# Plain first-layer units for six block units, six H tiles, and another order of second-layer products in a fused attention and mixture kernel

## The chip, the core and the metric

The kernel runs on one core of a Trainium2 chip. The metric is the device time of one execution in microseconds. Five runs of the kernel before gave a median of 374.88 us, from 374.55 to 375.29. One execution was also recorded by the hardware profiler; the profile and the trace are of that one.

## The reference: what is computed

Two stages follow each other. The first is attention of 4 batches x 8 heads x 768 positions x 64, where each query sees the first 4 positions (the sink) and a window of the last 128 positions. The second is a mixture of 4 experts over the 3072 tokens: each expert is a two-layer network 512 -> 1024 -> 512, and its output is weighted with a normalised gate.

```python
scores = np.where(is_sink | in_window, scale * q @ k.T, -1e9)
x = softmax(scores) @ v                 # then heads side by side: [3072, 512]
p = domain_probs / domain_probs.sum(-1)
for e in range(4):
    out += p[:, e:e + 1] * (np.maximum(x @ w1[e], 0.0) @ w2[e])
```

## The kernel before, in words

**Tiling.** Tokens are worked on in groups of 256 (three groups for each batch, `NG = 3`). A *unit* is the first layer of one expert on one group: 48 units in all. Its result is a tile `H` (1024 hidden values x 256 tokens in bf16).

**A plain unit** (`emit_first`, L1001) has four steps. A step is eight matmuls of 128 x 128 weights on 256 token columns into one PSUM bank, `hps`; then one VectorE instruction (L1025) applies ReLU and the gate. In batch 0, L1014 on ScalarE or L1016 on VectorE does the ReLU alone.

**A block unit** (`emit_fast`, L1078) does the same with seven block products P1 to P7 in place of eight, in the manner of Strassen and Winograd: each is eight matmuls of 128 x 128 weights on 128 columns, into `cps`, so 56 in all. It works with sums and differences of weight blocks (`weight_form1`, L319 to L325, four VectorE instructions for each expert, once) and of token blocks (`tokens`, L1052). Its partial results are copied by ScalarE (L1106, L1119), added by VectorE (L1113, L1128) and gated by VectorE (L1097, four times). `START` says from which batch on an expert uses block units: expert 0 from batch 1, expert 1 from batch 2, experts 2 and 3 in batch 3. That makes 21 block units and 27 plain ones.

**The second layer** in batch 0 is plain (L1286). In batches 1 to 3 it too is done in seven block products for each group (`emit_product`, L1218). A product consists of one *piece* for each expert, four matmuls of 256 columns each; so a group's chain is 28 pieces. The products of a group come in the order of `CHAIN`. Two PSUM banks `acc` are used: P1, P6, P7 and P4 go to bank 0, P2, P5 and P3 to bank 1. Behind a product its bank is copied or added to the output tile `osb` by ScalarE (L1259) or VectorE (L1250, L1255), and P1 is copied to bank 1 (L1247). `S` holds the sums of H blocks that P5 and P6 need (L1178, three VectorE instructions for each unit), and L1157 forms the operand of P3. Each half of the output rows is stored by one DMA on SP's queue (L1236, L1252).

**What sets the order.** The kernel is written out by a planner that runs at build time: it keeps estimated times of the engines, and the loop at L1344 chooses the next TensorE work among those that are ready, by a priority number (lower first): attention that is due 0, otherwise 3; first-layer steps 2 (L1386); a product piece 1 or 2.5 (L1385). In before a piece gets 1 when VectorE is estimated to be more than `BEHIND` = 800 ns behind. Work of VectorE and ScalarE goes through a list with deadlines (`later`, `flush`).

**H tiles.** There are six H tiles (`NH`). When the last batch's attention is out, `widened` (L897) makes three more from the tile `qkT`, which the attention no longer needs. A tile is given back as soon as its expert's piece of the chain's last product is out (L1224). `room` tells whether another unit may be opened.

**Attention.** Scores of two head pairs go out in one burst when four of six PSUM banks are free (`two`, L777, with `PAIR = 1`), and sink scores of two query groups in one burst (L570, with `ONE = 2`).

Of the kernel before, what the change touches and what calls it, by code (L numbers as in the profile page):

```python
# [16 lines left out]
def kernel(  # L17
# [12 lines left out]
    nc = tc.nc  # L30
# [27 lines left out]
    ]  # L58

    NGATE = 5  # L60
    START = {0: 1, 1: 2, 2: 3, 3: 3}
    ONACT = 1
    ONE = 2
    PAIR = 1
    BEHIND = 800
    BIASED = 1
    FAST = tuple(START)
    UNITS = ("P1", "P5", "P6", "P2", "P7", "P3", "P4")
# [235 lines left out]
    def weight_form1(e):  # L304

        w = w1_sb[e].rearrange("p (k d) (m f) -> p m k d f", k=2, m=2)
        A11, A12, A21, A22 = w[:, 0, 0], w[:, 0, 1], w[:, 1, 0], w[:, 1, 1]
        if e not in forms1:
            if START[e] < B - 1:
                x = wpool.tile([P, 3, NDB // 2, F // 2], BF16, name=f"vf_{e}", tag=f"vf_{e}")  # L310
                x = [x[:, i] for i in range(3)]
            else:
                x = [sb.tile([P, 2, H, D], BF16, name="qkn", tag="qkn", bufs=NQB) for _ in range(3)]
                x = [i.rearrange("p d h c -> p d (h c)") for i in x]
            forms1[e] = {"P1": A11, "P2": A12, "P3": x[2], "P4": A22, "P5": x[0], "P6": x[1], "P7": A21}
            formed1[e] = 0
        x = forms1[e]
        if formed1[e] == 0:
            nc.vector.tensor_add(x["P5"], A21, A22)  # L319
        elif formed1[e] == 1:  # L320
            nc.vector.tensor_sub(x["P6"], x["P5"], A11)
        elif formed1[e] == 2:
            nc.vector.tensor_sub(x["P3"], A12, x["P6"])
        else:
            nc.vector.tensor_sub(A21, A11, A21)  # L325
        formed1[e] += 1
        forms1_at[e] = dve(1024, rate=1.92)
# [3 lines left out]

    def form1_due(e):
        n = formed1.get(e, 0)
        if START[e] == B - 1 and turned_at.get((B - 1, NQB - 1), 1e12) > t["pe"]:
            return False
        return landed.get(("w1", e), 1e12) < t["pe"] and (n < 3 or n == 3 and not left1[e])

    def form_due(e):
# [516 lines left out]
    NH = 6  # L855
    QF = NFB // 2
    PAIRS = [(b, g) for b in range(1, B) for g in range(NG)]
    CHAIN = ("P1", "P2", "P6", "P5", "P7", "P3", "P4")
    acc_free = [0.0, 0.0]
    out_sb = {}  # L860

    class Mixture:


        def __init__(self):
            self.early = {g: list(range(E)) for g in range(NG)}
# [12 lines left out]
            self.H, self.H_at, self.H_part = {}, {}, {}  # L879
            self.S, self.S_at, self.waiting, self.last = {}, {}, [], []  # L880
            self.products = [(b, g, m) for b, g in PAIRS for m in CHAIN]
            self.piece, self.chores = 0, 0
            self.at, self.S4_at, self.C22 = {}, {}, {}
            self.done = 0.0
            self.stored = []
            self.spare, self.lent = [], {}

        def is_fast(self, b, e):
            return b >= START.get(e, B)
# [1 line left out]
        def more(self):  # L891
            return bool(self.open or any(self.early.values()) or self.units or self.second or self.products)

        def room(self):
            return self.spare or self.live < NH

        def widened(self):  # L897

            x = sb.tile([P, 2, NHP, S], BF16, name="qkT", tag="qkT", bufs=1)
            x = x.rearrange("p i h n -> p (i h n)")  # L900
            n = 2 * QF * 2 * P
            self.spare = [x[:, i * n:(i + 1) * n].rearrange("p (k f t n) -> p k f t n", k=2, f=QF, t=2) for i in range(3)]

        def early_ready(self, g):
            if not self.early[g] or not self.room():
                return 1e12
            xs = [xT_at.get((0, hp, g), 1e12) for hp in range(NHP)]
            e = self.early[g][0]
            return max([t["pe"], free_at(), landed.get(("w1", e, 0), landed.get(("w1", e), 1e12)), *xs])

        def opened(self, b, g, e):

            if self.spare:
                self.H[b, g, e] = self.spare.pop()
                self.lent[b, g, e] = self.H[b, g, e]
            else:
                self.H[b, g, e] = mo.tile([P, 2, QF, 2, P], BF16, name="H", tag="H", bufs=NH)
                self.live += 1
            fast = self.is_fast(b, e)

            def complete(at):
                self.H_at[b, g, e] = at
                self.finished.add((b, g, e))
                if b:
                    self.waiting.append((b, g, e))
                    load_gates()

            self.H_part[b, g, e] = join(4, complete)
            return {"unit": (b, g, e), "fast": fast, "left": list(UNITS) if fast else list(range(QF)), "at": {}}

        def begin(self):

            if self.open or any(self.early.values()):
                return
            if self.units and self.room():
                self.open.append(self.opened(*self.units.pop(0)))

        def widen(self):

            u = self.open[0]  # L940
            if len(self.open) == 1 and u["unit"][0] and len(u["left"]) < len(UNITS) and self.units and self.room():
# [195 lines left out]
        def chore(self):  # L1137
# [11 lines left out]

            if self.last:  # L1150
                b, g, e = u = self.last[0]
                if (b, g, "P2") not in self.products:
                    self.last.pop(0)

                    def form(engine):
# [53 lines left out]
        def emit_product(self):  # L1209
# [11 lines left out]
                )  # L1221
            end = pe(QF * G, ready, n=QF)
            self.piece = (k + 1) % E
            if m == CHAIN[-1]:  # L1224
                if (b, g, e) in self.lent:
                    self.spare.append(self.lent.pop((b, g, e)))
                else:
                    self.live -= 1
            if k < E - 1:
                return  # L1230
            self.products.pop(0)
            if m == "P1":
                out_sb[b, g] = mo.tile([P, 2, Dout], FP32, name="osb", tag="osb", bufs=1)
                r = (b * NQB + 2 * g) * P
                def store(at):
                    nc.sync.dma_start(out=out[r + P:r + 2 * P, :], in_=out_sb[b, g][:, 1])  # L1236
                    sp(at)
                self.C22[b, g] = join(2, store)
            o = out_sb[b, g]
            C11, C12, C21, C22 = o[:, 0, 0:G], o[:, 0, G:], o[:, 1, 0:G], o[:, 1, G:]  # L1240
            acc_free[bank], seeded = 1e12, acc_free[1]
            if m == "P1":
                acc_free[1] = 1e12

            def run(engine):
                if m == "P1":
                    nc.scalar.copy(out=acc[1][:, 0:G], in_=x)  # L1247
                    acc_free[0] = acc_free[1] = act(G, seeded)
                elif m == "P3":
                    nc.vector.tensor_add(C12, C12, x)  # L1250
                    acc_free[1] = at = dve(G)
                    nc.sync.dma_start(out=out[r:r + P, :], in_=o[:, 0])  # L1252
                    sp(at)
                elif m == "P7":
                    nc.vector.tensor_add(C22, C22, x)  # L1255
                    acc_free[0] = at = dve(G)
                    self.C22[b, g](at)
                else:
                    nc.scalar.copy(out={"P2": C11, "P6": C12, "P5": C22, "P4": C21}[m], in_=x)  # L1259
                    acc_free[bank] = at = act(G)  # L1260
                    if m == "P4":
                        self.C22[b, g](at)
            r = (b * NQB + 2 * g) * P
            later("dve" if m in ("P3", "P7") else "act", end, 200, run)

        def second_ready(self):
            if not self.second:
# [53 lines left out]
    ahead, upto, loaded, wide = 0, 0.0, 0, 0  # L1321
# [22 lines left out]
    while mix.more() or att.more():  # L1344
        now = t["pe"]

        if not att.more() and ahead == B - 1 and not wide:
            wide = 1
            mix.widened()
        if not att.more() and not loaded:  # L1350
            loaded = 1
            gates_by_row()
# [28 lines left out]
        if att.more():  # L1381
            opts = [(max(r, now), (0 if due else 3) - 0.1 * (step == "two"), "att", step) for r, step in att.options()]
        s2, p = mix.second_ready(), mix.product_ready()
        behind = max(t["dve"] - now, 0.0) + 500 * sum(x[2] == "dve" and x[0] < now + 300 for x in pend)
        opts.append((max(p, now), 1 if behind > BEHIND else 2.5, "product", None))  # L1385
        opts += [(max(f, now), 2, "first", x) for f, x in mix.firsts()]  # L1386
        opts.append((max(s2, now), 1 if mix.since >= 1 else 2.5, "second", None))
        soonest = min(o[0] for o in opts)
# [58 lines left out]
```

The softmax here doesn't subtract the row's maximum and nothing guards it: scores larger than these inputs give would overflow.

## Time and profile before

| what | us |
|---|---|
| median of five runs | 374.88 |
| the profiled execution | 374.97 |
| its span, first to last instruction | 373.3 |
| TensorE busy / VectorE busy / ScalarE busy | 362.7 / 285.2 / 153.1 |
| L1001, plain first layer, 864 matmuls, busy | 107.0 |
| L1078, block first layer, 1176 matmuls, busy | 79.2 |
| L1218, second-layer products, 1008 matmuls, busy | 127.3 |
| last first-layer matmuls start | 349.73 |
| last DMA issued | 370.33 |

Times in the trace are counted from the start of the span. "PE" is TensorE's matmuls, "PEld" its weight loads, which overlap them, "DVE" VectorE, "ACT" ScalarE and "POOL" GpSimd. A busy time of a matmul is longer than the step from one matmul to the next, since matmuls are pipelined; the pace is read from starts. A bracket at the end of a timeline line tells how long the engine was idle before it and who ended that. In the view by windows, the columns are: the window, its length, then busy time and instructions of each engine, the granted TensorE clock, the DMA share and GB/s.

Attention runs beside the mixture until about 253 us; its last score burst starts at 240.84. From 281.5 to 350.2 come the first-layer units of batch 3 mixed with second-layer products, and from 350.17 second-layer products alone. The span ends 3.0 us after the last DMA is issued.

### The profile page before, as it was taken

The numbers are of one execution on the slowest core, as the hardware profiler recorded it, in microseconds if no ns is written. First come the engines' busy times: TensorE is split into PE (matmuls) and PEld (weight loads), VectorE is DVE, ScalarE is ACT, GpSimd is POOL, SyncE is SP. The second block draws the span as 40 slices with busy tenths as digits, with TensorE's granted clock in tenths as the row PEclk, the third lists the DMA queues.
The fourth block names the chain that finished last, engine by engine and source line by source line (L and its number), as shares of the span: only waits on it lengthen the run. The fifth ranks groups of instructions, "written<-read, shape, count | busy, mean of one in ns | idle before, by whom it ended". The sixth has DMA issues, their size and how long they took to land.

```text
span 373.3 us, 9793 instructions
## 1 busy us (share of the span) xinstructions
PE 362.7 (97%) x4096; PEld 300.2 (80%) x4096; DVE 285.2 (76%) x630; ACT 153.1 (41%) x396; POOL 71.1 (19%) x91
## 2 busy tenths in 40 slices
PE   6899999999999999999999999999999999999996
PEld 3575766667667788889987998899999999999975
DVE  5674997675553899778879789779899889899930
ACT  4764733675565226445336145543103222222110
POOL 8935112808131191001020000000000000000000
PEclk9999999999999999999999999999999999999999
DMA  9999999939999999027991023114012111110011
GB/s 164 165 189 199 210 211 177 149 25 119 136 129 211 159 139 129 30 70 73 167 147 43 3 64 80 41 45 86 16 30 72 30 44 58 31 59 2 2 56 58
DMA packets 110808, 35.63 MB, mean 95 GB/s; under 512 B 94260, under 2 KB 106132, under 8 KB 110764
## 3 DMA queue, kind: packets, MB, share of 16 engines
q0 software_dynamic: 77520, 17.31, 52.1%
q1 hardware_dynamic: 32188, 17.18, 20.8%
q8 instruction: 32, 0.52, 0.6%
q10 hardware_dynamic: 1056, 0.52, 0.5%
q14 instruction: 12, 0.10, 0.1%
HBM read 40.45 MB, written 6.34 MB: 125 GB/s over the span
## 4 chain that ended last, share of the span: by engine, by line
PE 88%; DVE 4%; ACT 4%; DMA 3%; issue 1%; ACTq 0%; DVEq 0%
PE acc L1218 29%; PE hps L1001 24%; PE cps L1078 17%; PE acc L1286 9%; PE sps L618 3%; PE od L684 2%; DMA xT<-onat 2%; DMA kraw<-in_k_dram 2%; PE tr L512 1%; ACT aT L643 1%; ACT onat L723 1%; PE od L677 1%; DVE H L1016 1%; DVE onat L714 1%; PE tx L742 1%
## 5 line engine op out<-in xcount | busy, mean ns | idle before, releaser
L1001 PE MATMUL hps<-xT,w 128*128 128x256 bf16 x864 | 107.0, 273 | 0.4 <-DVE H L1016 0.3
L1001 PEld LDWEIGHTS <-w 128*128 128x128 bf16 x864 | 82.2, 98 | 13.3 <-issue 2.5
L1218 PEld LDWEIGHTS <-H 128*128 128x128 bf16 x600 | 56.1, 98 | 7.6 <-issue 1.9
L643 ACT ACTIVATE aT<-sps 128x512 bf16<-128x512 f32 (+1 forms) x96 | 47.1, 576 | 30.7 <-PE sps L618 30.6
L723 ACT ACTIVATE onat<-od,R 128x64 bf16<-128x64 f32 x144 | 33.3, 331 | 39.7 <-DVE R L711 39.7
L1218 PE MATMUL acc<-w,H 128*128 128x256 bf16 x360 | 47.7, 272 | 1.0 <-ACT osb L1259 0.5
L1025 DVE SCALAR_TENSOR_TENSOR H<-hps,gates 128x512 bf16<-128x512 f32 x56 | 38.2, 689 | 12.4 <-PE hps L1001 12.2
L1286 PE MATMUL acc<-w,H 128*128 128x512 bf16 x192 | 45.4, 379 | 0.0
L1078 PEld LDWEIGHTS <-w 128*128 128x128 bf16 x672 | 42.5, 98 | 1.9 <-issue 0.5
L254 POOL DMA_DIRECT2D vx<-in_v_dram x24 | 21.4, 901 | 75.2 <-PE od L684 66.4
L1259 ACT COPY osb<-acc 128x256 f32<-128x256 f32 x36 | 13.6, 384 | 52.8 <-PE acc L1218 51.9
L1097 DVE SCALAR_TENSOR_TENSOR H<-cps,gates 128x512 bf16<-128x512 f32 x48 | 32.9, 687 | 2.1 <-PE cps L1078 1.3
L1286 PEld LDWEIGHTS <-H 128*128 128x128 bf16 x192 | 18.3, 98 | 17.5
L1218 PE MATMUL acc<-wf,H 128*128 128x256 bf16 x240 | 31.9, 273 | 0.0
L1014 ACT ACTIVATE H<-hps 128x512 bf16<-128x512 f32 x35 | 20.9, 598 | 24.2 <-PE hps L1001 23.8
L1218 PEld LDWEIGHTS <-S 128*128 128x128 bf16 x288 | 27.0, 98 | 3.8 <-issue 1.1
L1106 ACT COPY cps<-cps 128x512 f32<-128x512 f32 x21 | 12.1, 576 | 42.2 <-PE cps L1078 40.5
L1298 DVE SCALAR_TENSOR_TENSOR osb<-acc,scale_t,osb 128x512 f32<-128x512 f32 x18 | 13.5, 750 | 16.9 <-PE acc L1286 16.9
L1078 PE MATMUL cps<-T,w 128*128 128x128 bf16 x336 | 25.6, 219 | 0.0
L1078 PE MATMUL cps<-xT,w 128*128 128x128 bf16 x336 | 25.3, 219 | 0.0
L189 POOL DMA_DIRECT2D qkn<-in_q_dram x22 | 20.0, 907 | 18.9 <-PE tr L512 9.2
L1078 PEld LDWEIGHTS <-vf 128*128 128x128 bf16 x360 | 22.5, 98 | 1.0 <-issue 0.2
(117 smaller groups left out, 523.8 us busy)
## 6 DMA issues: line engine op xcount, KB each, us to landing
w<-in_moe_w_dram POOLq DMA_DIRECT2D x7, 1024.0 KB, 18.9
out_dram<-osb SPq DMA_DIRECT2D x24, 256.0 KB
gates<-gate_rows SPq DMA_DIRECT2D x36, 128.0 KB
vx<-in_v_dram POOLq DMA_DIRECT2D x24, 128.0 KB, 5.9
qkn<-in_q_dram POOLq DMA_DIRECT2D x22, 128.0 KB, 6.4
qkn<-in_k_dram POOLq DMA_DIRECT2D x22, 128.0 KB, 6.4
w<-in_moe_w_dram POOLq DMA_DIRECT2D x2, 512.0 KB, 8.8
kraw<-in_k_dram ACTq DMA_DIRECT2D x2, 256.0 KB
```

Source lines behind the costliest of these rows:

```text
L189: nc.gpsimd.dma_start(out=both[:, i], in_=src[b, :, tb * P:(tb + 1) * P, :].rearrange("h p d -> p h d"),)
L254: nc.gpsimd.dma_start(out=vx[tb][:, :, 0:D], in_=v[b, :, tb * P:(tb + 1) * P, :].rearrange("h p d -> p h d"),)
L643: nc.scalar.activation(out=a[:, ph], in_=sps[ph][:, 0:w], func=AF.Exp, scale=scale)
L723: nc.scalar.mul(o[:, qi, hp, ph * D:(ph + 1) * D], od[:, qi, ph, 0:D], R[:, qi, ph])
L1001: nc.tensor.matmul(h[:, i].rearrange("p (q n) -> p q n", q=2), lhsT=w1_sb[e][:, db, fb * P:(fb + 1) * P], rhs=xT[b, g][:, :, db], start=(i ...
L1014: nc.scalar.activation(out=dst, in_=h, func=AF.Relu)
L1025: nc.vector.scalar_tensor_tensor(out=dst, in0=h, scalar=0.0, in1=gate, op0=ALU.max, op1=ALU.mult,)
L1078: nc.tensor.matmul(y[:, f], lhsT=A[:, d, f * P:(f + 1) * P], rhs=T[:, d], start=(m in ("P1", "P5") and f == 0 and d == 0), stop=(d == 1), ...
L1097: nc.vector.scalar_tensor_tensor(out=dst, in0=src, scalar=0.0, in1=gate, op0=ALU.max, op1=ALU.mult)
L1218: nc.tensor.matmul(x, lhsT=self.operand(b, g, e, m)[:, f], rhs=forms[e][m][:, f], start=(k == 0 and f == 0 and m in ("P1", "P5")), stop=(k ...
L1259: nc.scalar.copy(out={"P2": C11, "P6": C12, "P5": C22, "P4": C21}[m], in_=x)
L1286: nc.tensor.matmul(op, lhsT=H[:, fb // QF, fb % QF, s], rhs=w2_sb[e][:, fb, :], start=(fb == 0), stop=(fb == NFB - 1),)
```

## The change

1. `START` keeps experts 0 and 1 alone. Experts 2 and 3 are plain in batch 3 as well: 15 block units and 33 plain ones. Their weight forms, and the code that put those in the `qkn` tiles, are gone.
2. `widened`, `spare` and `lent` are gone: six H tiles throughout. All four tiles of a group are given back when the group's P3 is out.
3. `CHAIN` ends P4, P3 instead of P3, P4. P5 is not evacuated by itself: its sum stays in bank 1, P7 is copied by ScalarE to the output's fourth block, and VectorE then adds bank 1 to that.
4. A product piece gets priority 1 when `mix.credit` is at least 1024. First-layer steps add to the credit (2048 for a plain step, 1024 for a block product) and each piece takes 1024 from it. The rule with `BEHIND` is gone.
5. The operand of P3 (L1157) is formed once P5 is out, instead of P2.

`PAIR`, `ONE`, `two`, `scores` and `sinks` are the same on both sides. The core of the diff:

```diff
-    START = {0: 1, 1: 2, 2: 3, 3: 3}
+    START = {0: 1, 1: 2}
-    BEHIND = 800
-    CHAIN = ("P1", "P2", "P6", "P5", "P7", "P3", "P4")
+    CHAIN = ("P1", "P2", "P6", "P5", "P7", "P4", "P3")
-        def room(self):
-            return self.spare or self.live < NH
-        def widened(self):
...
-            self.spare = [x[:, i * n:(i + 1) * n].rearrange(...) for i in range(3)]
-            if self.units and self.room():
+            if self.units and self.live < NH:
...
-                if (b, g, "P2") not in self.products:
+                if (b, g, "P5") not in self.products:
...
-            if m == CHAIN[-1]:
-                if (b, g, e) in self.lent:
-                    self.spare.append(self.lent.pop((b, g, e)))
-                else:
-                    self.live -= 1
+            if m == "P5":
+                acc_free[1] = end
+                return
...
-                elif m == "P7":
-                    nc.vector.tensor_add(C22, C22, x)
-                    acc_free[0] = at = dve(G)
-                    self.C22[b, g](at)
-                else:
-                    nc.scalar.copy(out={"P2": C11, "P6": C12, "P5": C22, "P4": C21}[m], in_=x)
-                    acc_free[bank] = at = act(G)
-                    if m == "P4":
-                        self.C22[b, g](at)
+                nc.scalar.copy(out={"P2": C11, "P6": C12, "P7": C22, "P4": C21}[m], in_=x)
+                acc_free[bank] = at = act(G)
+                if m == "P4":
+                    sp(at)
+                    self.C22[b, g](at)
+                if m == "P7":
+                    def add(engine):
+                        nc.vector.tensor_add(C22, C22, acc[1][:, 0:G])
+                        acc_free[1] = dve(G)
+                        self.C22[b, g](acc_free[1])
+                    acc_free[1] = 1e12
+                    later("dve", at, 300, add)
...
+            if m == "P3":
+                self.live -= E
...
-        behind = max(t["dve"] - now, 0.0) + 500 * sum(x[2] == "dve" and x[0] < now + 300 for x in pend)
-        opts.append((max(p, now), 1 if behind > BEHIND else 2.5, "product", None))
+        opts.append((max(p, now), 1 if mix.credit >= QF * G else 2.5, "product", None))
```

More of the change, by code (lines that the diff above doesn't have):

```diff
@@ L308, in weight_form1 @@
         if e not in forms1:
-            if START[e] < B - 1:
-                x = wpool.tile([P, 3, NDB // 2, F // 2], BF16, name=f"vf_{e}", tag=f"vf_{e}")
-                x = [x[:, i] for i in range(3)]
-            else:
-                x = [sb.tile([P, 2, H, D], BF16, name="qkn", tag="qkn", bufs=NQB) for _ in range(3)]
-                x = [i.rearrange("p d h c -> p d (h c)") for i in x]
-            forms1[e] = {"P1": A11, "P2": A12, "P3": x[2], "P4": A22, "P5": x[0], "P6": x[1], "P7": A21}
+            x = wpool.tile([P, 3, NDB // 2, F // 2], BF16, name=f"vf_{e}", tag=f"vf_{e}")
+            forms1[e] = {"P1": A11, "P2": A12, "P3": x[:, 2], "P4": A22, "P5": x[:, 0], "P6": x[:, 1], "P7": A21}
             formed1[e] = 0
@@ L333, in form1_due @@
         n = formed1.get(e, 0)
-        if START[e] == B - 1 and turned_at.get((B - 1, NQB - 1), 1e12) > t["pe"]:
-            return False
         return landed.get(("w1", e), 1e12) < t["pe"] and (n < 3 or n == 3 and not left1[e])
@@ L885, in __init__ @@
             self.stored = []
-            self.spare, self.lent = [], {}
         def is_fast(self, b, e):
@@ L892, in more @@
             return bool(self.open or any(self.early.values()) or self.units or self.second or self.products)
-        def room(self):
-            return self.spare or self.live < NH
-        def widened(self):
[L899 to L902, printed above, removed]
         def early_ready(self, g):
-            if not self.early[g] or not self.room():
+            if not self.early[g] or self.live >= NH:
                 return 1e12
@@ L911, in opened @@
         def opened(self, b, g, e):
-            if self.spare:
-                self.H[b, g, e] = self.spare.pop()
-                self.lent[b, g, e] = self.H[b, g, e]
-            else:
-                self.H[b, g, e] = mo.tile([P, 2, QF, 2, P], BF16, name="H", tag="H", bufs=NH)
-                self.live += 1
+            self.H[b, g, e] = mo.tile([P, 2, QF, 2, P], BF16, name="H", tag="H", bufs=NH)
+            self.live += 1
             fast = self.is_fast(b, e)
@@ L940, in widen @@
             u = self.open[0]
-            if len(self.open) == 1 and u["unit"][0] and len(u["left"]) < len(UNITS) and self.units and self.room():
+            if len(self.open) == 1 and u["unit"][0] and len(u["left"]) < len(UNITS) and self.units and self.live < NH:
                 b, g, e = self.units[0]
@@ L1223, in emit_product @@
             self.piece = (k + 1) % E
-            if m == CHAIN[-1]:
-                if (b, g, e) in self.lent:
-                    self.spare.append(self.lent.pop((b, g, e)))
-                else:
-                    self.live -= 1
             if k < E - 1:
@@ L1234, in emit_product @@
                 r = (b * NQB + 2 * g) * P
[L1235 to L1238, printed above, removed]
+                self.C22[b, g] = join(2, lambda at: nc.sync.dma_start(out=out[r + P:r + 2 * P, :], in_=out_sb[b, g][:, 1]))
             o = out_sb[b, g]
             C11, C12, C21, C22 = o[:, 0, 0:G], o[:, 0, G:], o[:, 1, 0:G], o[:, 1, G:]
+            if m == "P5":
+                acc_free[1] = end
+                return
             acc_free[bank], seeded = 1e12, acc_free[1]
@@ L1248, in run @@
                     acc_free[0] = acc_free[1] = act(G, seeded)
-                elif m == "P3":
+                    return
+                if m == "P3":
                     nc.vector.tensor_add(C12, C12, x)
@@ L1253, in run @@
                     sp(at)
-                elif m == "P7":
-                    nc.vector.tensor_add(C22, C22, x)
-                    acc_free[0] = at = dve(G)
-                    self.C22[b, g](at)
-                else:
-                    nc.scalar.copy(out={"P2": C11, "P6": C12, "P5": C22, "P4": C21}[m], in_=x)
-                    acc_free[bank] = at = act(G)
-                    if m == "P4":
-                        self.C22[b, g](at)
+                    return
+                nc.scalar.copy(out={"P2": C11, "P6": C12, "P7": C22, "P4": C21}[m], in_=x)
+                acc_free[bank] = at = act(G)
+                if m == "P4":
+                    sp(at)
+                    self.C22[b, g](at)
+                if m == "P7":
[5 more added lines that the diff above has]
+                    later("dve", at, 300, add)
             r = (b * NQB + 2 * g) * P
-            later("dve" if m in ("P3", "P7") else "act", end, 200, run)
+            later("dve" if m == "P3" else "act", end, 200, run)
+            if m == "P3":
+                self.live -= E
         def second_ready(self):
@@ L1320 @@
     work = [E * NG * 2 * NFB * NDB * G] + [NG * E * NFB * G * (NDB + 7 / 4) - NG * sum(mix.is_fast(b, e) for e in FAST) * NFB * P for b in range(1, B)]
-    ahead, upto, loaded, wide = 0, 0.0, 0, 0
+    ahead, upto, loaded = 0, 0.0, 0
     loads, turns = [(load_nat, 0, tb) for tb in (4, 5)] + [(load_v, 0, (4, 5))], []
@@ L1345 @@
         now = t["pe"]
-        if not att.more() and ahead == B - 1 and not wide:
-            wide = 1
-            mix.widened()
         if not att.more() and not loaded:
```

## The prediction, made before the result was known

> **What bounds the kernel now.** I read the page's busy shares first, then what TensorE waited for from the first second-layer product on (130 us), then the stretch in which the edited units run (282 to 350 us), and last the end.
>
> ```profile
> PE 362.7 (97%) x4096; PEld 300.2 (80%) x4096; DVE 285.2 (76%) x630; ACT 153.1 (41%) x396; POOL 71.1 (19%) x91
> PE 88%; DVE 4%; ACT 4%; DMA 3%; issue 1%; ACTq 0%; DVEq 0%
> ```
>
> TensorE is busy for 97% of the span and holds 88% of the chain that ended last. A modelled busy share could hide gaps, so the next view is its waits in 130:373.3:
>
> ```profile
> PE acc L1218 <- ACT osb L1259: 1.0, 2, 0.5
> PE acc L1218 <- ACT acc L1247: 0.4, 1, 0.4
> ```
>
> Three waits, 1.4 us in 243 us. All that can be won from waiting there is small. Now the pace, from start times of consecutive matmul groups in the timeline (columns: start, busy, engine, line):
>
> ```profile
> 266.58 1.91 PE L1001 MATMUL hps<-xT,w 128*128 128x256 bf16 x16
> 268.33 0.60 PE L1218 MATMUL acc<-w,S 128*128 128x256 bf16 x4
> ...
> 340.00 0.61 PE L1078 MATMUL cps<-T,w 128*128 128x128 bf16 x8
> 340.45 0.61 PE L1078 MATMUL cps<-T,qkn 128*128 128x128 bf16 x8
> ```
>
> Sixteen 256-column matmuls take 268.33 - 266.58 = 1.75 us, 109.3 ns each; eight of 128 columns take 0.445 us (the chain has 16 in 0.89), 55.7 ns each. The stretch 281.50:350.34 holds all first-layer work of batch 3, twelve block units (L1078), and second-layer products (L1218); one line for each source:
>
> ```profile
> 281.50:350.34 68.84, 43.71 (x672) 40.57 (x671) 1.00 0.11 37
> 281.50:350.34 68.84, 37.22 (x288) 26.48 (x287) 1.00 0.11 37
> ```
>
> 672 = 12 units x 56, and 672 x 55.7 + 288 x 109.3 = 37.4 + 31.5 = 68.9 us against 68.84 measured. So this stretch is matmul columns end to end, at a granted clock of 1.00. VectorE is busy for 62.06 of 68.34 us in 282:350.34, but TensorE never waits for it there.
>
> **Block units of experts 2 and 3 in batch 3 become plain.** START loses those two, so 2 experts x 3 groups = 6 units change. A block unit has 7 products x 8 matmuls of 128 columns: 56 x 55.7 = 3.12 us. A plain unit has 4 steps x 8 matmuls of 256: 32 x 109.3 = 3.50 us. TensorE gets 6 x 0.38 = **+2.25 us**, in a stretch that has no idle to take it up. This term I hold certain to about 0.1.
>
> VectorE loses work: a block unit has 4 gatings (L1097, 0.687) and two adds (L1113 0.692, L1128 0.685), 4.13 us; a plain one 4 gatings (L1025, 0.689), 2.76; so 6 x 1.37 = 8.2 us. ScalarE loses 6 x (0.576 + 0.594) = 7.0 us (L1106, L1119). The eight weight forms of experts 2 and 3 go too: 8 x 0.69 = 5.5 us, six of them at 192 to 206 us. Nothing waits for VectorE behind 282 us, so I price its relief there at zero; the work that hides it is the matmuls themselves. Around the six forms TensorE is busy for 9.44 of 10 us in 200:210, the weakest slice in mid-kernel; that slice also has one filler matmul (L1086, 0.215 us at its measured 215-ns step). So between 0 and -0.8 us; I take 0, because the attention's score burst and its exponentials, which stay, are in the same slice.
>
> **A rule that speaks against this.** For the row of 55.7 ns, the Trainium skill (TensorE: Matmul & The Clock Gate, Back-to-back issue gap) gives about 81 ns for each 128-column matmul in a sustained stream of weight loads and matmuls. By it, as an estimate, a block unit would take 56 x 81 = 4.5 us against my 3.5 for a plain one, and the edit would win 6 us, not lose 2. The trace has 672 of them in the stretch above, at a pace that leaves no room for 81; the measurement decides.
>
> **Products: order, banks and priority.** The chain's end P7, P3, P4 becomes P7, P4, P3; P5 stays in bank 1 until P7's ScalarE copy is followed by a VectorE add of it. Counts stay: five ScalarE evacuations and two VectorE adds for each group of tokens, two stores of 256 KB, swapped in order on SP's queue. What moves is who waits for a bank when nothing else lies between. The end of before shows both kinds:
>
> ```profile
> 356.49 0.37 ACT L1259 COPY osb<-acc 128x256 f32<-128x256 f32 x1 [4.87 <-PE acc L1218]
> 356.91 1.91 PE L1218 MATMUL acc<-w,H 128*128 128x256 bf16 x16 [0.46 <-ACT osb L1259]
> 358.85 0.36 ACT L1247 COPY acc<-acc 128x256 f32<-128x256 f32 x1 [1.99 <-PE acc L1218]
> 359.26 1.91 PE L1218 MATMUL acc<-w,H 128*128 128x256 bf16 x16 [0.44 <-ACT acc L1247]
> ```
>
> The first wait is P4 of one group, then P1 of the next, both in bank 0: 0.46 us, and it goes, as P3 (bank 1) will lie between. The second, P1 to P2, stays. New is P7 to P4 in bank 0: about 0.44 us whenever the chain runs alone, once for certain in the last group. VectorE's add of P5 has P4's 1.75 us to finish in, against 0.42 for one add, and P3 queues behind it only if VectorE is over a microsecond late. Net 0 for one exposed chain; up to 9 x 0.44 = 4 us if all nine were exposed. Before 350 us other matmuls lie between, so I take 0 and keep the 4 for the range. The last evacuation is now a VectorE add, 0.42 instead of 0.37: nothing.
>
> Products now come first when first-layer credit is there, instead of when VectorE is behind. With TensorE full this changes the order of the same matmuls, not their number; score bursts and sink bursts have the same code on both sides (PAIR and ONE are not in the diff), so the bursts change only by where banks happen to be free: two 6-matmul bursts for one 12-matmul burst cost 2 x 0.33 against 0.55, 0.1 us each, either sign.
>
> **The H buffers and the end.** Before has three more H tiles behind the attention (written as qkT, first read at 283.7) and gives one back with each piece of the chain's last product. After has six, and gives four back when P3 of the group is out. So in the last batch two units of the next group can be open while a chain runs; the other two come after its P3. For the middle groups the freed four tiles also admit the group after, so TensorE has work. For the last group there is none: experts 1 (block) and 3 (plain) run when chain 8 of 9 is done, with only the P1 pieces of experts 0 and 2 beside them, and P1's last piece waits for the last gating. In before that moment is covered by 12 pieces' worth of older products:
>
> ```profile
> 349.73 0.61 PE L1078 MATMUL cps<-T,w 128*128 128x128 bf16 x8
> 350.17 1.04 PE L1218 MATMUL acc<-w,S 128*128 128x256 bf16 x8
> 350.38 0.69 DVE L1097 SCALAR_TENSOR_TENSOR H<-cps,gates 128x512 bf16<-128x512 f32 x1 [0.25 <-PE cps L1078]
> ```
>
> The gating ends 351.07 - 350.17 = 0.90 us behind the last first-layer matmul. In after at most a piece of P1 (0.44) hides it: at least 0.46 us of new idle. Above: VectorE in these two units has 4.13 + 2.76, perhaps six S forms of the earlier two units (2.52) and two output adds (0.83), 10.2 us, against 3.12 + 3.50 + 0.87 of TensorE; idle of 10.2 + 0.9 - 7.5 = 3.6 us. I take **+1.2**, nearer the lower row, since with an even fuller VectorE the gating came 0.21 us behind its product.
>
> **Sum.** Profiled execution 374.97 us (span 373.3), 0.09 over the median of 374.88: 374.97 + 2.25 + 1.2 + 0 + 0 = **378.4 us**.
>
> **Rivals.**
> - *Starvation by six tiles* (chance 0.19): four tiles given back at once also stalls the middle groups, and chains run alone. Price: 0.44 and up to about 0.9 us for each of nine groups, 4 to 12 us less what is counted: 381 to 387. For it: the tiles are cut in just the batch with the fullest engines. Against it: batches 1 and 2 of before live with six tiles and TensorE has no such waits there.
> - *Faster by the order* (0.04): products set between first-layer steps take away TensorE's idle at 130 to 350 and at the end. Its whole price is bounded by the profile: 1.4 us of waits, 2.1 + 1.8 us of weight-load issue gaps (score lines and products), 0.5 in 200:210; about 5.8 us, so at best 371.5. It decides only from 2.25 + 0.75 us recovered; most of the issue gaps sit at score bursts, which stay.
> - *No change* (0.06): no end stall, and 1.5 us or more of that idle gone: 374.2 to 375.6.
> - *The title's bursts* are already what before does, so that part can give nothing; it is in the forecast.
>
> **Numbers.** Forecast case 0.71 (376.8 to 381). Below 376.5 lie the last two rivals, above 382.5 about half of starvation: range 376.5 to 382.5. About 0.2% (0.75 us) is what can be told from no change; faster 0.04, same 0.06, slower 0.90.
>
> **What would show it.** L1001 goes from 864 to 1056 matmuls and L1078 from 1176 to 840. L319, L321, L323 and L325 fall from four to two each. In the wait view, an idle of about 0.4 us before P4 in the last chain and 0.5 to 3.6 us before its P1's last piece; that last stretch should hold some 28 pieces behind the last first-layer matmul, not 40. VectorE's share falls by some 13 us in all. I am wrong if the products' line shows many waits from 130 to 350, or if plain units take over 110 ns a matmul.

## The result, and the profile after

The changed kernel takes 375.93 us (median of 27 runs, 374.81 to 376.65); the kernel before, run beside it, 375.05 (45 runs). The ratio is 1.0023, with a 95% interval of 1.0017 to 1.0030: slower by 0.9 us. The forecast was 378.4 us with 376.5 as the low end, so the direction was right and the size was four times too large. The profiled execution took 375.66 us, with a span of 374.0 where before had 373.3.

From the page of after: the busy shares, and the shares of the chain that ended last.

```profile
PE 364.1 (97%) x3951; PEld 299.6 (80%) x3951; DVE 269.4 (72%) x610; ACT 146.9 (39%) x384; POOL 71.3 (19%) x91
PE 89%; DVE 4%; DMA 3%; ACT 2%; issue 0%; ACTq 0%; DVEq 0%
```

TensorE still sets the end. VectorE lost 15.8 us of work (13.7 were counted), ScalarE 6.2 (7.0). The groups of the first layer, L978 (L1001 of before) and L1055 (L1078 of before), have the counts that were expected, 1056 and 480 + 360 = 840; their lines as the page has them:

```profile
L978 PE MATMUL hps<-xT,w 128*128 128x256 bf16 x1056 | 130.6, 273 | 0.4 <-DVE H L993 0.3
...
L1055 PEld LDWEIGHTS <-w 128*128 128x128 bf16 x480 | 30.6, 98 | 1.5 <-issue 0.5
...
L1055 PEld LDWEIGHTS <-vf 128*128 128x128 bf16 x360 | 22.6, 98 | 0.6
```

The waits of TensorE behind 130 us in after (who waited, for whom, us, times, longest):

```profile
PE acc L1195 <- ACT osb L1228: 0.5, 1, 0.5
PE acc L1195 <- ACT acc L1219: 0.4, 1, 0.4
```

Two waits of 0.9 us, where before had three of 1.4. One of before's, 0.54 us at 204.84, was not at the end but in mid-kernel. The windows 180:210 and 200:210 (length, busy time and count of PE, PEld, DVE, ACT and POOL, granted clock, DMA share, GB/s), first of before, then of after:

```profile
180.00:210.00 30.00, 29.44 (x326) 25.49 (x325) 24.73 (x59) 12.51 (x42) 2.62 (x3) 1.00 0.77 103
200.00:210.00 10.00, 9.44 (x107) 8.26 (x108) 8.07 (x19) 6.13 (x21) 0.00 (x0) 1.00 0.05 16
```

```profile
180.00:210.00 30.00, 30.00 (x348) 26.79 (x346) 22.50 (x59) 11.80 (x40) 2.63 (x3) 1.00 0.75 102
200.00:210.00 10.00, 10.00 (x117) 9.12 (x115) 6.01 (x19) 5.28 (x19) 0.00 (x0) 1.00 0.06 16
```

The slice that was TensorE's weakest is full in after, with 22 matmuls more in 30 us. That is where part of the forecast loss went. Not all of it is gain: a burst of attention work moved out of this slice too, as the account shows.

**An account that all runs share.** A 256-column matmul is shown busy for 273 ns but the next can start 109 ns behind it, so busy times hide gaps up to some 0.16 us. So I also counted starts in each trace: from the first second-layer product to the last matmul, the sum of the steps that matmuls take without a gap (109.2 ns for 256 columns, 55.8 for a block product's 128, 215 for the filler, 56 for a transpose, 29 or 57 for the attention's values, 33.5 for a score) and the rest, called *idle*. It holds the bursts' own gaps and the sink bursts (four matmuls each, 0.4 us, for which no step is taken off). The steps are counts times a pace; what a trace adds is the idle. The column "sink burst" says when the second of two such bursts starts. All in us:

| run | first product | steps | idle | of it at 180 to 210 | at 180 to 240 | at 270 to 360 | behind 360 | sink burst | last matmul to end | span |
|---|---|---|---|---|---|---|---|---|---|---|
| before | 135.2 | 227.9 | 6.5 | 2.1 | 3.1 | 1.4 | 0.0 | 199.6 | 3.6 | 373.3 |
| after | 135.1 | 229.9 | 5.2 | 0.6 | 2.4 | 0.6 | 0.6 | 211.7 | 3.7 | 374.0 |
| e1 plain only | 135.5 | 229.9 | 6.2 | 0.8 | 2.4 | 1.2 | 0.6 | 212.4 | 3.7 | 375.3 |
| e2 credit only | 135.5 | 228.2 | 11.8 | 1.8 | 3.9 | 4.1 | 1.4 | 199.8 | 3.6 | 379.0 |
| e3 chain only | 135.2 | 227.9 | 7.7 | 1.8 | 2.9 | 2.2 | 0.6 | 200.2 | 3.7 | 374.6 |
| e4 six tiles only | 135.6 | 227.9 | 8.0 | 2.1 | 3.1 | 2.3 | 0.6 | 200.1 | 3.6 | 375.2 |
| e5 plain, forms kept | 135.3 | 230.2 | 7.0 | 2.1 | 3.1 | 1.2 | 0.6 | 199.8 | 3.6 | 376.1 |
| e6 forms late | 135.0 | 227.7 | 5.9 | 0.8 | 2.5 | 1.4 | 0.0 | 211.9 | 3.6 | 372.2 |
| e7 after, BEHIND | 134.2 | 229.9 | 8.9 | 2.1 | 3.2 | 2.4 | 1.2 | 198.7 | 3.7 | 376.7 |
| e8 after, steps turned | 135.6 | 229.9 | 6.0 | 0.6 | 2.3 | 1.4 | 0.6 | 212.1 | 3.7 | 375.3 |
| e9 plain and credit | 134.5 | 230.4 | 6.0 | 1.8 | 3.3 | 0.7 | 0.0 | 198.9 | 3.6 | 374.5 |
| e10 after, block | 135.8 | 227.9 | 11.7 | 1.6 | 3.0 | 4.0 | 2.8 | 200.5 | 3.7 | 379.1 |
| e11 after, chain of before | 136.5 | 230.4 | 6.0 | 1.8 | 3.4 | 0.1 | 0.6 | 200.8 | 3.7 | 376.5 |

The first product moves by a microsecond or two between profiled executions (134.2 to 136.5), so a single span says less than the medians below. Before to after: steps +2.0 (six units, +2.2, less one filler matmul of 0.215), idle -1.3, of which 0.8 at 180 to 240.

One pattern runs through the table. Where the sink burst starts at 198 to 201 us, 180 to 240 holds 2.9 to 3.9 us of idle; where it starts at 211 to 213 us (after, e1, e6, e8), 2.3 to 2.5. The six runs that form the weight sums of experts 2 and 3 at 192 to 216 us (before, e2, e3, e4, e5, e10) all have the early burst, but so have e7, e9 and e11, which form none. So leaving these sums out is not enough to be rid of that idle.

### The profile page after: what moved, and what is told of

It reads as the page before. It is cut to its first block, busy times and chain, and to the rows that moved or that the text cites. A ratio compares the mean times of both kernels' runs of the same rounds, so it can differ in the third digit from the quotient of the medians.

```text
span 374.0 us, 9430 instructions
## 1 busy us (share of the span) xinstructions
PE 364.1 (97%) x3951; PEld 299.6 (80%) x3951; DVE 269.4 (72%) x610; ACT 146.9 (39%) x384; POOL 71.3 (19%) x91
## 3 DMA queue, kind: packets, MB, share of 16 engines
q10 hardware_dynamic: 1056, 0.52, 0.5%
## 4 chain that ended last, share of the span: by engine, by line
PE 89%; DVE 4%; DMA 3%; ACT 2%; issue 0%; ACTq 0%; DVEq 0%
PE acc L1195 30%; PE hps L978 29%; PE cps L1055 13%; PE acc L1265 9%; PE sps L610 3%; PE od L676 2%; DMA kraw<-in_k_dram 2%; DMA xT<-onat 2%; PE tr L504 1%; ACT aT L635 1%; PE od L669 1%; DVE H L993 1%; DVE onat L706 1%; PE tx L734 1%; DVE aT L644 0%
## 5 line engine op out<-in xcount | busy, mean ns | idle before, releaser
L978 PE MATMUL hps<-xT,w 128*128 128x256 bf16 x1056 | 130.6, 273 | 0.4 <-DVE H L993 0.3
L978 PEld LDWEIGHTS <-w 128*128 128x128 bf16 x1056 | 99.7, 98 | 14.9 <-issue 2.5
L1195 PEld LDWEIGHTS <-H 128*128 128x128 bf16 x720 | 68.2, 98 | 9.2 <-issue 2.0
L1002 DVE SCALAR_TENSOR_TENSOR H<-hps,gates 128x512 bf16<-128x512 f32 x84 | 57.1, 689 | 2.7 <-PE hps L978 2.5
L1195 PE MATMUL acc<-w,H 128*128 128x256 bf16 x432 | 56.3, 273 | 0.4 <-ACT acc L1219 0.4
L1195 PE MATMUL acc<-wf,H 128*128 128x256 bf16 x288 | 35.2, 273 | 0.5 <-ACT osb L1228 0.5
L1265 PEld LDWEIGHTS <-H 128*128 128x128 bf16 x192 | 18.3, 98 | 17.5
L1055 PEld LDWEIGHTS <-w 128*128 128x128 bf16 x480 | 30.6, 98 | 1.5 <-issue 0.5
L1074 DVE SCALAR_TENSOR_TENSOR H<-cps,gates 128x512 bf16<-128x512 f32 x45 | 30.7, 686 | 0.9 <-PE cps L1055 0.7
L629 DVE TENSOR_TENSOR aT<-aT,mask 128x1024 bf16<-128x1024 bf16 (+1 forms) x36 | 22.7, 642 | 10.2 <-ACT aT L635 10.2
L1083 ACT COPY cps<-cps 128x512 f32<-128x512 f32 x15 | 8.7, 582 | 47.6 <-PE cps L1055 45.4
L1055 PEld LDWEIGHTS <-vf 128*128 128x128 bf16 x360 | 22.6, 98 | 0.6
L188 POOL DMA_DIRECT2D qkn<-in_k_dram x22 | 20.0, 911 | 8.6 <-DMA w<-in_moe_w_dram 8.5
```

The costliest lines, as they stand in the source:

```text
L188: nc.gpsimd.dma_start(out=both[:, i], in_=src[b, :, tb * P:(tb + 1) * P, :].rearrange("h p d -> p h d"),)
L629: nc.vector.tensor_mul(a, a, m[:, None, :].to_broadcast([P, 2, w]))
L978: nc.tensor.matmul(h[:, i].rearrange("p (q n) -> p q n", q=2), lhsT=w1_sb[e][:, db, fb * P:(fb + 1) * P], rhs=xT[b, g][:, :, db], start=(i ...
L1002: nc.vector.scalar_tensor_tensor(out=dst, in0=h, scalar=0.0, in1=gate, op0=ALU.max, op1=ALU.mult,)
L1055: nc.tensor.matmul(y[:, f], lhsT=A[:, d, f * P:(f + 1) * P], rhs=T[:, d], start=(m in ("P1", "P5") and f == 0 and d == 0), stop=(d == 1), ...
L1074: nc.vector.scalar_tensor_tensor(out=dst, in0=src, scalar=0.0, in1=gate, op0=ALU.max, op1=ALU.mult)
```

## The experiments

Each was timed beside the kernel before, so all ratios are to before; at 375 us a difference of 0.001 is 0.4 us.

**e1, `START` alone.**

```diff
-    START = {0: 1, 1: 2, 2: 3, 3: 3}
+    START = {0: 1, 1: 2}
```

> Before with START of after alone: six block units of batch 3 become plain and the eight weight forms of experts 2 and 3 go; order rule, chain, nine H tiles stay. Theory A (the 1.3 us of matmul idle that after has less than before from 125 us on comes from the VectorE work that START takes away, mainly the forms at 192 to 206 us): columns +2.2 and idle -1.3, so +0.9 us, ratio 1.0025, and the wait before the product at 204 us is gone. Theory B (it comes from the order of products): the full +2.2 us, ratio 1.006, with the idle of before still there. Both: the stretch with first-layer work of batch 3 is longer by 2.2 us.

Measured 1.0045 (1.0028 to 1.0061), +1.7 us, between the two theories. The account splits it: steps +2.0, idle at 180 to 210 us down by 1.3 as theory A has it, but 0.6 of that is idle again at 210 to 240 us, where the sink and score bursts now lie, and 0.6 more stands at the end, where P1 to P2 of the last two groups are exposed (waits of 0.44 and 0.45 us) instead of one.

**e2, the credit rule alone.**

```diff
-        opts.append((max(p, now), 1 if behind > BEHIND else 2.5, "product", None))
+        opts.append((max(p, now), 1 if mix.credit >= QF * G else 2.5, "product", None))
```

> Before with the credit rule for a product's priority in place of BEHIND, nothing else. Theory A: 0 within 0.5 us, ratio 0.9985 to 1.0015. Theory B, with the priority rule as the part that matters: -1.3 us, ratio 0.9965, the waits at 199 to 207 and at 231 us gone though the forms are still made there.

Measured 1.0143 (1.0122 to 1.0164), +5.4 us. Neither theory had this. TensorE's longest waits behind 130 us in this run:

```profile
PE cps L1078 <- DVE cps L1113: 3.0, 5, 0.8
PE cps L1078 <- DVE H L1128: 0.5, 1, 0.5
PE acc L1218 <- ACT acc L1247: 0.4, 1, 0.4
...
```

Block products (L1078) wait five times for the VectorE add that seeds P7 and P3 (L1113), at 293 to 340 us, and once at 363 us for the add before P4 (L1128). In before no block product waits for VectorE at all, though VectorE is busy for 91% of that stretch (62.06 of 68.34 us). The longest wait, in the timeline of this run: VectorE has two gatings (L1097) ahead of the add, and TensorE has no product piece to put before the block product that waits.

```profile
330.25 0.68 DVE L1097 SCALAR_TENSOR_TENSOR qkT<-cps,gates 128x512 bf16<-128x512 f32 x1
...
330.86 0.68 DVE L1097 SCALAR_TENSOR_TENSOR qkT<-qkT,gates 128x512 bf16<-128x512 f32 x1
331.45 0.69 DVE L1113 TENSOR_TENSOR cps<-qkT,cps 128x512 f32<-128x512 f32 x1
...
332.19 0.61 PE L1078 MATMUL cps<-T,w 128*128 128x128 bf16 x8 [0.80 <-DVE cps L1113]
```

The BEHIND rule sends a product piece just when VectorE is estimated to be behind; the credit rule sends it by a count. Behind 270 us stand 4.1 of the 5.3 us of idle that this run has more than before.

**e3, the chain alone.** The order P7, P4, P3 in before, with P5 left in bank 1 and added behind P7's copy, and L1157 formed once P5 is out.

```diff
-    CHAIN = ("P1", "P2", "P6", "P5", "P7", "P3", "P4")
+    CHAIN = ("P1", "P2", "P6", "P5", "P7", "P4", "P3")
...
```

> Before with the chain P7, P4, P3 and P5 left in bank 1, nothing else. Both theories expect the end to be worth nothing: the 0.46 us before P1 of the last group goes, one of about 0.45 us comes between P7 and P4 of it. Theory A: 0 within 0.5 us in all, ratio 0.9985 to 1.0015. Theory B with the chain as the part that matters: -1.3 us, ratio 0.9965. If P7 to P4 is exposed in each of nine groups: +4 us, ratio 1.011.

Measured 1.0033 (1.0018 to 1.0049), +1.2 us: more than nothing. TensorE waits for the copy in L1258 (this run's line of the copies to `osb`) three times, at 331, 354 and 367 us: the wait of P4 for P7's copy is exposed in three groups, not in the last one alone.

```profile
PE acc L1218 <- ACT osb L1258: 1.4, 3, 0.5
```

**e4, six tiles alone.** `widened` is never called; tiles are still given back piece by piece.

```diff
-        if not att.more() and ahead == B - 1 and not wide:
+        if not att.more() and ahead == B and not wide:
```

> Before with six H tiles to the end (widened is never called), still given back piece by piece, nothing else. The prediction's end term had +1.2 us (0.46 to 3.6) for this. Rival, from the trace of after: P1 reads one of the four blocks of H, which is gated early, so no idle arises at the last group: 0 within 0.5 us, ratio 0.9985 to 1.0015. Starvation would show as +2 us or more, with waits between 280 and 350 us.

Measured 1.0037 (1.0022 to 1.0053), +1.4 us: the size of the prediction's end term. The timeline of this run shows where most of it is (0.82 us):

```profile
358.16 0.61 PE L1078 MATMUL cps<-xT,qkn 128*128 128x128 bf16 x8
358.52 0.41 DVE L1178 TENSOR_TENSOR S<-S,H 128x512 bf16<-128x512 bf16 x1
358.85 0.68 DVE L1128 TENSOR_TENSOR H<-H,cps 128x512 f32<-128x512 f32 x1
359.45 0.68 DVE L1097 SCALAR_TENSOR_TENSOR H<-cps,gates 128x512 bf16<-128x512 f32 x1
359.59 0.61 PE L1078 MATMUL cps<-T,w 128*128 128x128 bf16 x8 [0.82 <-DVE H L1128]
```

The last block unit's P4 waits 0.82 us for its own add on VectorE. That is the wait inside a block unit, not the one for the last gating that the prediction had named, and two waits of 0.4 and 0.2 us for the add that seeds P7 and P3 (L1113) come at 311 and 336 us.

**e5, `START` alone with six of the forms kept.** Experts 2 and 3 are plain, but their sums P5, P6 and P3 are still formed at 192 to 206 us, into tiles that nothing reads.

```diff
-            return b >= START.get(e, B)
+            return b >= START.get(e, B) and e < 2
...
-        return landed.get(("w1", e), 1e12) < t["pe"] and (n < 3 or n == 3 and not left1[e])
+        return landed.get(("w1", e), 1e12) < t["pe"] and (n < 3 or n == 3 and START[e] < B - 1 and not left1[e])
```

> As the run with START of after alone, but VectorE still makes six of the eight weight forms of experts 2 and 3 (sums that nothing reads). If the forms made the idle at 180 to 210 us: that idle is back (2.1 us instead of 0.8), ratio to before 1.007 to 1.009. If it came from the other order that START brings: as without them, idle 0.8, ratio 1.0045.

Measured 1.0074 (1.0053 to 1.0095), as the forms theory said. The idle at 180 to 210 is 2.1 us again, the sink burst is back at 199.75, and the window 200:210 is that of before:

```profile
200.00:210.00 10.00, 9.45 (x109) 8.18 (x106) 8.16 (x20) 6.29 (x22) 0.00 (x0) 1.00 0.06 16
```

**e6, the forms later.** In before, the forms of experts 2 and 3 wait until the last attention is out.

```diff
-        if START[e] == B - 1 and turned_at.get((B - 1, NQB - 1), 1e12) > t["pe"]:
+        if START[e] == B - 1 and (ahead < B - 1 or att.more()):
```

> Before with the forms of experts 2 and 3 made when the last attention is out (behind about 253 us) and no longer at 192 to 206. Theory that the forms there make the idle: 180 to 210 us holds 0.8 us of idle instead of 2.1, ratio 0.997, a kernel faster than both. Rival (they are not the cause, or VectorE is too full behind 253 us and the first block units of experts 2 and 3 wait for them): ratio 0.9985 or more, with idle moved to 280 to 300 us.

Measured 0.9973 (0.9963 to 0.9983), 374.17 us beside 375.25: faster than before and than after, and as expected. Of the 1.0 us, 0.2 is the filler matmul, which is not in this run. The forms now lie at 253 to 264 us; TensorE's first read of one comes at 293.66. Windows 200:210 and 210:240:

```profile
200.00:210.00 10.00, 10.00 (x124) 8.66 (x122) 8.45 (x18) 4.63 (x15) 0.00 (x0) 1.00 0.07 19
210.00:240.00 30.00, 29.82 (x383) 26.10 (x380) 23.82 (x53) 15.10 (x42) 0.00 (x0) 1.00 0.18 47
```

How this comes about is only in part seen. In the timeline of before, TensorE waits at 204.84 for the copy that frees a product's bank. ScalarE has output scalings, exponentials and a sink exponential in one heap ahead of that copy, and a form stands among VectorE's work there:

```profile
199.60 0.40 PE L579 MATMUL sinks<-qkT,ksd 128*32 128x512 bf16 x4
...
199.98 0.40 PE L618 MATMUL sps<-qkT 64*128 64x128 bf16 x6
...
202.05 1.17 ACT L643 ACTIVATE aT<-sps 128x512 bf16<-128x512 f32 x2
202.07 0.69 DVE L319 TENSOR_TENSOR qkn<-w 128x1024 bf16<-128x1024 bf16 x1
...
203.00 0.71 ACT L587 ACTIVATE sinkA<-sinks 128x512 bf16<-128x512 f32 x1
...
203.48 1.04 ACT L723 ACTIVATE onat<-od,R 128x64 bf16<-128x64 f32 x4
...
204.26 0.80 ACT L1259 COPY osb<-acc 128x256 f32<-128x256 f32 x2
204.84 1.03 PE L1218 MATMUL acc<-w,S 128*128 128x256 bf16 x8 [0.54 <-ACT osb L1259]
```

The forms are not needed for the heap: e9, which has none, has the sink exponential at 202.28, four output scalings at 202.76 and the copy at 203.54. What is shown is the effect of the edits: with the order rule of before, forms at 192 to 206 us cost about 1 us. But each time the planner also orders its work anew: in e6 the sink burst lies at 211.86 and the score burst behind it is gone from 199.98, in e5 both are back. Whether the sums' own time on VectorE counts, or only the order that the planner makes of them, these runs do not tell, for none moves the burst alone.

**e7, after with the BEHIND rule.**

```diff
-        opts.append((max(p, now), 1 if mix.credit >= QF * G else 2.5, "product", None))
+        behind = max(t["dve"] - now, 0.0) + 500 * sum(x[2] == "dve" and x[0] < now + 300 for x in pend)
+        opts.append((max(p, now), 1 if behind > 800 else 2.5, "product", None))
```

> After with the BEHIND rule for products in place of the credit, nothing else. In before the credit rule cost 5.4 us, with waits of block products for VectorE's adds. If the credit is as bad in after, this is faster than after by several us, ratio to before below 1.000. If plain units take that cost away: between after (1.0023) and START alone (1.0045), 1.002 to 1.005.

Measured 1.0120 (1.0102 to 1.0138), 379.91 us: slower than after by 3.6 us by the ratios, outside what I had for either case. Idle is 8.9 us against 5.2 (in a profiled execution that was the shortest of its six). TensorE's longest waits in this run:

```profile
PE acc L1195 <- ACT osb L1228: 2.3, 5, 0.5
PE acc L1195 <- ACT acc L1219: 0.7, 2, 0.4
...
```

The five waits, at 271, 297, 323, 349 and 369 us, come once for each of the last five groups: P4 behind P7 in bank 0. VectorE is busy for 53.01 of 68 us at 282 to 350 here, against 61.93 in before. So, as I read the rule, it seldom finds VectorE behind and sends pieces only when nothing else is ready; the chain's end runs alone, and the wait that the prediction priced at 0.44 us for each exposed group is there. In after the credit puts first-layer steps between, and it is exposed once. Most of the rest of the idle is at 180 to 210 (2.1 instead of 0.6), with the sink burst at 198.67 and no forms made.

**e8, after with the last group's plain steps turned.**

```diff
-            return {..., "left": list(UNITS) if fast else list(range(QF)), "at": {}}
+            return {..., "left": list(UNITS) if fast else [2, 3, 0, 1] if (b, g) == PAIRS[-1] else list(range(QF)), "at": {}}
```

> After, with the four steps of the plain units of the last group of tokens in the order 2, 3, 0, 1, so that the block of H that P1 reads is gated last and not first. My reading that P1 needs this block alone: TensorE now waits for the last gating before P1's last piece, 0.4 to 1.0 us at 358 us, where after has no wait; ratio to before 1.0035 to 1.005. Rival (P1 waits for the whole unit in any case): as after, 1.0023, no new wait.

Measured 1.0045 (1.0030 to 1.0060), 0.8 us more than after. The wait that the prediction forecast for the change is there, made by the turn:

```profile
357.43 1.04 PE L978 MATMUL hps<-xT,w 128*128 128x256 bf16 x8
357.82 0.69 DVE L1002 SCALAR_TENSOR_TENSOR H<-hps,gates 128x512 bf16<-128x512 f32 x1
358.31 0.82 PE L1195 MATMUL acc<-w,H 128*128 128x256 bf16 x6
...
359.02 0.68 DVE L1002 SCALAR_TENSOR_TENSOR H<-hps,gates 128x512 bf16<-128x512 f32 x1
...
359.76 0.39 PE L1195 MATMUL acc<-w,H 128*128 128x256 bf16 x2 [0.64 <-DVE H L1002]
```

**e9, two parts: `START` and the credit rule, in before.** The diffs of e1 and e2 together.

> Before with two parts of the change: START of after and the credit rule; chain and nine H tiles stay. Alone they cost 1.7 and 5.4 us. If the credit's cost comes from block units of batch 3 that wait for VectorE's adds, it is gone here: ratio 1.001 to 1.004, no waits of block products behind 280 us. If the two costs add: 1.019.

Measured 1.0042 (1.0030 to 1.0054): just above the first case, and far from 1.019. No block product waits in it. So the credit rule's cost is one of block units in batch 3: with plain ones it adds nothing to e1's 1.0045.

**e10, after with block units again** (the four experts' `START` and the eight forms, in the `qkn` tiles as in before).

```diff
-    START = {0: 1, 1: 2}
+    START = {0: 1, 1: 2, 2: 3, 3: 3}
...
```

> After with block units for experts 2 and 3 in batch 3 again (and their eight forms), order, chain and six H tiles of after. Columns alone: 2 us less than after, ratio to before 0.997. If block units wait for VectorE under the credit rule: 4 to 7 us of idle behind 280 us and 1.3 us at 180 to 210 us, ratio 1.010 to 1.017.

Measured 1.0147 (1.0134 to 1.0161), 4.7 us slower than after although its steps are 2.0 us shorter. Its longest waits (L1062, L1097 and L1112 of this run are L1055, L1090 and L1105 of after):

```profile
PE cps L1062 <- DVE cps L1097: 3.3, 5, 0.8
PE acc L1202 <- ACT acc L1226: 0.6, 2, 0.4
PE cps L1062 <- DVE H L1112: 0.5, 1, 0.5
...
```

The same wait as in e2, five times, 3.3 us: block products for the add on VectorE. In the order of after, plain units are the cheaper ones. The forms, now at 199 to 208 us, bring the sink burst back to 200.5 and the idle at 180 to 240 to 3.0.

**e11, after with the chain of before** (P7, P3, P4; P5 evacuated by itself).

```diff
-    CHAIN = ("P1", "P2", "P6", "P5", "P7", "P4", "P3")
+    CHAIN = ("P1", "P2", "P6", "P5", "P7", "P3", "P4")
...
```

> After with the chain P7, P3, P4 and P5 evacuated by itself, as in before; credit rule, plain units and six tiles (given back behind P4). My account has the swap as worth nothing while other matmuls lie between: ratio to before 1.001 to 1.004, the wait of 0.46 us at 366 us gone and one before P1 of a later group in its place. If the chain is what saves after: 1.006 or more.

Measured 1.0045 (1.0032 to 1.0058), 0.8 us more than after, just above the first case. The wait at the end did go (0.7 us of idle behind 330 us instead of 1.2), but 1.8 us of idle stand at 180 to 210, as in e9, though no forms are made there. Why the orders without forms (after and e1 with 0.6 and 0.8; e9 and e11 with 1.8, e7 with 2.1) differ there was not tried further: in e9 and e11 values, sinks and scores come close together at 199 to 201 us, which happens or not by the planner's choices.

## Why the prediction was wrong, point by point

The forecast lay 2.7 us above the profiled execution. By the account 0.2 of that is the units, 1.3 the idle that went, 1.2 the end that did not come. The first is small; the other two are steps that failed.

- **TensorE's columns set the time: right.** In all thirteen profiles TensorE's steps fill what is not in the idle column, 5.2 to 11.8 us.
- **Six units, +2.25 us: right.** The step sums differ by 2.0, and by 2.2 without the filler matmul. That the pace held shows in what is left over at 270 to 330 us: 0.2 us of idle in before, none in after. e10 has the shorter steps beside a much larger wait.
- **VectorE's relief priced at zero, with -0.8 as its bound: wrong.** The step that failed reads "I take 0, because the attention's score burst and its exponentials, which stay, are in the same slice". They did not stay: before has the sink burst at 199.60 and a score burst at 199.98; after has the sink burst at 211.65 and the next score burst at 214.29. The prediction had the bursts change "only by where banks happen to be free", but the planner places them anew. Idle in the trace fell by 1.3 us, 0.8 of it at 180 to 240; the bound counted the slice 200:210 alone. Moving the six forms alone is worth 1.0 us (e6), and keeping them in e1's kernel costs 1.1 (1.0074 against 1.0045, e5; the two intervals overlap). That the forms' time on VectorE is the cause in after is not shown: e7, e9 and e11 are without forms as well and have the idle.
- **Product order and banks, net 0: right for this change as a whole**, since the wait before P1 of the last group (0.46) went and one of 0.46 before P4 came, as forecast:

```profile
358.89 0.36 ACT L1219 COPY acc<-acc 128x256 f32<-128x256 f32 x1 [6.41 <-PE acc L1195]
359.29 1.91 PE L1195 MATMUL acc<-w,H 128*128 128x256 bf16 x16 [0.44 <-ACT acc L1219]
...
366.48 0.37 ACT L1228 COPY osb<-acc 128x256 f32<-128x256 f32 x1 [3.12 <-PE acc L1195]
...
366.90 1.91 PE L1195 MATMUL acc<-wf,H 128*128 128x256 bf16 x16 [0.46 <-ACT osb L1228]
```

  Its reason was too short: other matmuls lie between in after only because of the credit rule (e7 against after), in before the chain alone costs 1.2 us (e3).
- **"With TensorE full this changes the order of the same matmuls, not their number": wrong as a reason.** Order alone made between -3.6 us (e7 to after) and +5.4 us (e2). It came out small here because the rule meets plain units (e9).
- **The end, +1.2 us (0.46 to 3.6): wrong, 0.** The step was "P1's last piece waits for the last gating". P1 reads one of the four blocks of H, which plain steps 0 and 1 fill; in after P1's last two pieces start at 357.81, when the last gating (358.53) is still to come, and end into the copy wait that was there before:

```profile
357.81 1.04 PE L1195 MATMUL acc<-w,H 128*128 128x256 bf16 x8
...
358.53 0.68 DVE L1002 SCALAR_TENSOR_TENSOR H<-hps,gates 128x512 bf16<-128x512 f32 x1
```

  Turned steps bring the wait, 0.64 us (e8). With block units six tiles did cost 1.4 us (e4), but that it is near the 1.2 is luck: its longest wait stands between the last unit's own P7 add and P4, and after has a plain unit last.
- **Rivals.** Starvation did not come: no wait of after lies between 130 and 350 us. (The upper end of its price, 387, leaves out the +2.25: 374.97 + 2.25 + 12 is 389.) The rival that was nearest is "no change", by its mechanism, idle of mid-kernel gone; its time of up to 375.6 was missed by 0.3. "Faster by the order" had a bound of 5.8 us, of which 1.3 went; it counts the wait at 204.84 twice, among the waits and as the 0.5 in 200:210.

The five edits are far from additive: four parts tried alone cost 1.7 + 5.4 + 1.2 + 1.4 = 9.7 us, and the change costs 0.9. What stays open: how much of the mid-kernel idle is order rather than the forms (after with the forms kept, or before with the sink burst moved alone, was not tried), and what giving four tiles back at once is worth, which was not tried by itself.

## What to carry to other kernels

Where one engine is full, count the columns of an edit first, but then ask of each piece of work that goes, and not only of each piece that comes, in which crowded stretch it lay: six optional instructions in the queue of an engine that is not the bound, moved by some 60 us, won a microsecond. Where a planner places the work, ask also what it will move in answer: work whose code is the same on both sides need not stay where it was. A rule that orders work is judged together with the units that it orders: the credit rule was 5.4 us worse with block units and 3.6 us better with plain ones and the new chain. And a consumer's wait is read from the part of the tile that it reads, not from the tile.

## What the runs showed of the hardware that was not expected

Block products on 128 columns kept a step of 55.8 ns with a 128 x 128 weight load of 98 ns each beside them, in streams of hundreds; the weight loads were busy for 65.0 of 68.34 us in before's last mixed stretch without holding a matmul up. The hand-over of a PSUM bank from a product through a copy of 0.37 us to the next product cost 0.44 to 0.46 us of idle where nothing lay between and ScalarE was free for the copy, in all thirteen profiles.
